# Chunk attention and token mixing: scores and mixing in quarters of the array, a permuted identity in E's transposes, steps and loads from a written table

## The chip, the core and the metric

The kernel runs on one core of a Trainium2 chip. The metric is the device time of one execution in microseconds (us); lower is better. A core has a matrix engine (TensorE, in the profile PE, its weight loads PEld), a vector engine (DVE), a scalar engine (ACT), GpSimd (POOL) and a queue engine (SP). Each runs its own instructions in order; semaphores order them among each other. PE writes only to PSUM, eight banks of 128 partitions by 512 words, from which DVE or ACT copy results to SBUF. Sixteen DMA engines carry data between the chip's memory and SBUF; here POOL issues the loads (they change float32 to float16 on the way), and SP issues the first two loads and all stores.

## What is computed

Per batch and head, attention inside chunks of 64 tokens, and then, per batch, a mixing of tokens whose weights come from the attention's output x (576 tokens, 512 columns):

```python
# q, k, v: (8 batches, 8 heads, 576 tokens, 64), chunks of 64 tokens
scores = scale * np.matmul(q_c, k_c.transpose(0, 1, 2, 4, 3))
scores = scores - np.max(scores, axis=-1, keepdims=True)
attn = np.exp(scores)
attn = attn / (np.sum(attn, axis=-1, keepdims=True) + 1e-09)
out = np.matmul(attn, v_c)
...
wq = x @ w_q
wk = x @ w_k
W_tok = scale * np.einsum('bsd,btd->bst', wq, wk)
mixed = np.einsum('bst,btd->bsd', W_tok, x)
return (np.maximum(mixed, 0.0) @ w_out).astype(np.float32)
```

The kernel never forms W_tok: with G = wk^T x (64 by 512 per batch), mixed is wq G.

## The kernel before

**Units.** A batch has 576 tokens: two *whole* units of 256 tokens (four chunks) and 64 tokens left over. The left-over chunks of two neighbouring batches, b and b + 1, form one *rest* unit. So there are 16 whole units and 4 rests, 20 in all, numbered in the order of `pairs`. Unit 0 is batch 0's first.

**Steps.** Each unit passes through the same steps; in brackets the line of the PE work, and the name that the table of the change gives it here.

- *Loads* (L263, L275, for rests L260, L271): q, k and v. A whole unit's q or k is one DMA of 256 KB (128 partitions, each with 8 heads and two neighbouring tokens); its v two of 128 KB. A rest has six DMAs of 64 KB.
- *Transposes of q and k* (tq, L402; rests L387): 16 per whole unit and tensor, 128 by 64 each, two column halves of the array side by side. They leave dims on partitions, two heads one above the other.
- *Copies*: k goes to `kt` in one copy. q goes to `qbd` in two copies of 64 partitions each, to the two diagonal blocks of a 128 by 128 tile whose other blocks were filled with zeros at the start. All simple copies carry line L318.
- *Scores* (S, L420): for each pair of heads and each chunk one matmul with the block-diagonal q as 128 by 128 weights and 64 columns of k; 16 per whole unit, 8 per rest.
- *Softmax*: maximum (mx, L433, DVE), subtraction (L444 or L440, DVE), exponent (L454, ACT). Two neighbouring tokens sit in one partition row after the load, so the keys come permuted; the subtraction's access pattern puts them back.
- *E* (L466): transposes of the exponents against an identity, then a copy `et`.
- *V* (L496): products with v, matmuls of 64 rows by 64 columns in quarters of the array, 65 columns of v with a column of ones that gives the sum. A whole unit has 32 in two groups that use four quarters; a rest has 16, each with its row half equal to its column half. Then DVE adds 1e-9, takes the reciprocal and multiplies (L508, L512, L522).
- *Projection*: transposes of x (xT, L538), product with w_q and w_k together (pj, L548), a transpose of wk (wkT, L565), each with a copy.
- *G* (L604), once per batch: ten matmuls over the batch's tokens, 128 by 64. Two copies put its halves side by side in rows 0 to 63 of `g16`, whose rows 64 to 127 are zero.
- *mix* (L645): four matmuls per whole unit with 128 by 128 weights out of `g16` and 256 columns (the lower half of the weights is the zeros). Then the relu (rm, L665 on ACT or L663 on DVE), whose access pattern puts the queries back in order.
- *out* (L679): product with w_out, four matmuls of 512 columns for each 128 tokens, a copy to `osb`, and the store (L693 to L699).

**Forms.** PE works in one of three forms: the full array, *tall* (128 rows by 64 columns: L402 and L604) and *quart* (64 by 64: L496). A change of form costs time.

**Order.** `plan` (L49) walks over all steps with a cost for each, a priority (unit number plus a lag for each kind, L163) and an estimate of when each load arrives. It picks for each engine what starts soonest, and gives each copy to DVE or ACT. The result is a fixed order on each engine. Where PE would wait early on, it inserts filler matmuls (`idle`, L712) with no use for the result, which keep PE busy and its clock up. Loads go out on POOL in the order of the units, q, k and v of each in turn, w_q and w_k after unit 1, w_out after unit 3. The order of the work on PE is thus fixed when the kernel is built; at run time an engine waits for whatever stands first on it.

## Time and profile before

| | |
|---|---|
| device time, median of three runs | 146.04 us (145.41 to 146.17) |
| span of the profiled execution, first to last instruction | 143.8 us |
| PE matmul, DVE, ACT, POOL busy | 127.5, 112.6, 101.3, 73.7 us |
| q0, loads issued by POOL: packets, MB | 78736, 14.29 |
| q1, loads and stores issued by SP: packets, MB | 7584, 10.49 |
| memory read, written | 29.62 MB, 9.44 MB |

The profile gives the span of the profiled execution only; the median of the runs shown lies 2.2 us above it. Columns of a row by line: line, engine, operation, output <- input, shapes, count; behind the bar the busy time in us and the mean of one in ns; behind the second bar the engine's idle time just before, and what ended it. Busy times of one engine can overlap a little (a matmul's latency runs into the next), so the distance from one start to the next tells more about PE than the mean of one. A DMA share above 1 means that packets wait for each other inside the sixteen engines.

### The profile page before, as it was taken

The page shows a single profiled execution, that of the slowest core. Times are in us where ns is not written, and L with a number is a line of the kernel's source. Part 1 is how long each engine was busy: PE and PEld are TensorE (multiplying, and loading weights), DVE is VectorE, ACT ScalarE, POOL GpSimd, SP SyncE. Part 2 cuts the span into 40 slices and gives each one's busy share as a digit, 9 for nine tenths or more (in the row PEclk, how much of TensorE's full clock was granted, in tenths as well). Part 3 has the DMA queues.
Part 4 walks back from the last instruction along what each step waited for, and adds up shares of the span by engine and source line. Part 5 has one row for each costly group of instructions (what it writes and reads, how often), then busy time and mean ns, then how long its engine had stood idle before and what let it go on. Part 6 is the DMA issues. An engine that isn't in the chain of part 4 may idle for free.

```text
span 143.8 us, 5196 instructions
## 1 busy us (share of the span) xinstructions
PE 127.5 (89%) x2204; PEld 90.8 (63%) x2204; DVE 112.6 (78%) x220; ACT 101.3 (70%) x182; POOL 73.7 (51%) x95
## 2 busy tenths in 40 slices
PE   5699799979799899998998999997999999997750
PEld 5565486566586776676675756786768766754310
DVE  6748988658989899897987899997999999933300
ACT  3333677457797899597978997867968687784740
POOL 7987997676499724551899526515960000000000
PEclk9999999999999999999999999999999999999998
DMA  3999999999999999999999999999999905527184
GB/s 88 268 176 155 129 165 184 169 175 175 156 133 173 234 218 175 208 247 239 86 151 195 216 241 207 213 257 168 125 181 229 270 22 152 140 75 197 31 250 111
DMA packets 86343, 25.11 MB, mean 175 GB/s; under 512 B 79152, under 2 KB 81712, under 8 KB 86320
## 3 DMA queue, kind: packets, MB, share of 16 engines
q0 software_dynamic: 78736, 14.29, 123.0%
q1 hardware_dynamic: 7584, 10.49, 23.7%
q8 instruction: 17, 0.28, 0.7%
q14 instruction: 6, 0.05, 0.1%
HBM read 29.62 MB, written 9.44 MB: 272 GB/s over the span
## 4 chain that ended last, share of the span: by engine, by line
PE 50%; DVE 15%; ACT 14%; DMA 10%; issue 4%; POOL 3%; POOLq 1%; ACTq 0%; DVEq 0%
PE ps L679 14%; PE ps L402 8%; DMA v_all<-in_v_dram 7%; PE ps L712 5%; PE ps L420 5%; DVE sh L444 4%; PE ps L496 4%; PE ps L538 4%; PE ps L548 3%; DVE qbd L318 3%; ACT qbd L318 3%; DMA osb<-in_q_dram 3%; ACT es L454 3%; PE ps L466 3%; DVE mx L433 2%
## 5 line engine op out<-in xcount | busy, mean ns | idle before, releaser
L679 PE MATMUL ps<-wo,rm 128*128 128x512 f16 x144 | 35.6, 379 | 0.7 <-ACT rm L665 0.7
L275 POOL DMA_DIRECT2D v_all<-in_v_dram x32 | 28.7, 912 | 3.1 <-DMA v_all<-in_v_dram 1.4
L433 DVE TENSOR_REDUCE mx<-ps 128x16 f32<-128x1024 f32 (+1 forms) x20 | 22.2, 1112 | 5.3 <-PE ps L420 4.2
L522 DVE TENSOR_TENSOR xs<-ps,rec 128x512 f16<-128x512 f32 x36 | 23.4, 685 | 0.1
L402 PE MATMUL ps<-ident,qk 128*64 128x128 f16 x512 | 20.7, 227 | 2.0 <-DVE qk L318 1.1
L318 ACT COPY osb<-ps 128x512 f32<-128x512 f32 x28 | 16.3, 586 | 7.9 <-PE ps L679 7.0
L454 ACT ACTIVATE es<-sh 128x1024 f16<-128x1024 f32 (+1 forms) x20 | 19.4, 970 | 3.2 <-DVE sh L444 1.7
L402 PEld LDWEIGHTS <-qk 128*64 128x64 f16 x512 | 16.4, 113 | 6.6 <-issue 3.7
L679 PEld LDWEIGHTS <-rm 128*128 128x128 f16 x144 | 12.6, 98 | 11.6 <-ACT rm L665 0.8
L444 DVE TENSOR_TENSOR sh<-ps,mx 128x1024 f32<-128x1024 f32 x16 | 19.6, 1223 | 0.4
L318 ACT COPY qbd<-ps 64x512 f32<-64x512 f32 (+1 forms) x30 | 15.9, 530 | 5.0 <-PE ps L402 3.0
L665 ACT ACTIVATE rm<-ps 128x1024 f16<-128x1024 f32 (+1 forms) x14 | 15.9, 1160 | 2.3 <-PE ps L645 2.3
L263 POOL DMA_DIRECT2D qk<-in_q_dram x15 | 13.6, 905 | 6.1 <-DMA qk<-in_q_dram 3.0
L263 POOL DMA_DIRECT2D qk<-in_k_dram x15 | 13.6, 906 | 5.1 <-DMA qk<-in_k_dram 5.1
L712 PE MATMUL ps<-ones 128*128 128x128 f16 (+1 forms) x72 | 13.8, 349 | 1.5 <-DVE ones L223 1.5
L420 PEld LDWEIGHTS <-qbd 128*128 128x128 f16 x288 | 10.8, 98 | 4.0 <-issue 1.8
L466 PE MATMUL ps<-ident,es 128*128 128x128 f16 x144 | 11.3, 219 | 1.9 <-ACT es L454 1.9
L420 PE MATMUL ps<-kt,qbd 128*128 128x64 f16 x288 | 11.6, 193 | 1.2 <-ACT kt L318 0.6
L538 PE MATMUL ps<-ident,xs 128*128 128x128 f16 x144 | 11.5, 219 | 0.4 <-DVE xs L522 0.4
L645 PE MATMUL ps<-wt,g 128*128 128x256 f16 (+1 forms) x96 | 10.6, 246 | 1.5 <-ACT g L318 1.0
L548 PE MATMUL ps<-xt,wqk 128*128 128x256 f16 (+1 forms) x80 | 11.2, 262 | 0.5 <-ACT xt L318 0.2
L271 POOL DMA_DIRECT2D v_all<-in_v_dram x8 | 5.4, 677 | 11.1 <-DMA qk<-in_k_dram 5.8
(54 smaller groups left out, 188.2 us busy)
## 6 DMA issues: line engine op xcount, KB each, us to landing
out_dram<-osb SPq DMA_DIRECT2D x40, 128.0 KB, 5.8
v_all<-in_v_dram POOLq DMA_DIRECT2D x32, 128.0 KB, 9.4
out_dram<-osb SPq DMA_DIRECT2D x16, 256.0 KB, 5.7
qk<-in_q_dram POOLq DMA_DIRECT2D x15, 256.0 KB, 8.5
qk<-in_k_dram POOLq DMA_DIRECT2D x15, 256.0 KB, 9.1
osb<-in_q_dram SPq DMA_DIRECT2D x1, 512.0 KB, 4.3
osb<-in_k_dram SPq DMA_DIRECT2D x1, 512.0 KB, 5.3
qk<-in_q_dram POOLq DMA_DIRECT2D x8, 64.0 KB, 8.9
```

The lines of the kernel that those rows point to most:

```text
L263: nc.gpsimd.dma_start(qk[u][:, t], rows)
L275: nc.gpsimd.dma_start(v_all[:, first[u] + i, :, 0:D], rows)
L318: (nc.vector.tensor_copy if eng == "DVE" else nc.scalar.copy)(to, of)
L402: nc.tensor.transpose(tp[half(o), j, :, r, :], of, ident[:])
L420: nc.tensor.matmul(sp[:, i, j, c, :], lhsT=st["qb", u][:, j, x].rearrange("p o s -> p (o s)"), rhs=st["kt", u][:, j, x * C : x * C + C], s ...
L433: nc.vector.tensor_reduce(mx[:], scores(), axis=AX.X, op=ALU.max)
L444: nc.vector.tensor_tensor(out=sh[:].rearrange("p x (g r) -> p x r g", r=R), in0=in_banks(bs, 512).rearrange("p i (x r g) -> p (i x) r g", ...
L454: nc.scalar.activation(es[:].rearrange("p x s -> p (x s)"), st["sh", u][:].rearrange("p x s -> p (x s)"), AF.Exp, scale=scale_attn,)
L522: nc.vector.tensor_tensor(out=to, in0=xp()[:, :, :, 0:D], in1=by, op=ALU.mult)
L538: nc.tensor.transpose(tx[:, f, i, :], xs[u][:, i, 2 * f : 2 * f + 2, :], ident[:])
L679: nc.tensor.matmul(op[c, :], lhsT=st["rm", u][:, f, i * P + c.start : i * P + c.stop], rhs=wo[:, f, :], start=(f == 0), stop=(f == NF - 1),)
L712: nc.tensor.matmul(ps[:, i, 0:cols], lhsT=ones[:, 0:P], rhs=ones[:, 0:cols], start=True, stop=True)
```

## The change

It touches almost every step. `plan`, its costs and its priorities are gone. In their place stand two texts. `ORDER` lists all 607 steps and the fillers, each with its engine (P for PE, V for DVE, S for ACT) and, for PE, the PSUM bank; `LOADS` lists POOL's loads. `w7` is a filler of 512 columns into bank 7, `n7` one of 128. Steps are numbered as they are added, unit by unit.

Ahead of unit 0's first transposes (7P0) stand 16 fillers, behind them 28 of w or n, so 44 in all:

```diff
+ORDER = """
+4V 5V 0S 1S w7 w7 w7 w7 n7 n7 n7 n7 n7 n7 n7 n7 n7 n7 n7 n7 7P0 2V 3S 8S w7 n7 n7 n7 n7 n7 n7 n7 n7
+9P1 10S 33P0 11P2 34V 12V 31P0 32S 13V w7 w7 n7 n7 n7 n7 n7 n7 n7 n7 55P0 35P4 56V 14S 36V 57P0 91P2
+15P3 92S 37V 89P6 16S 90S 58V 38S w2 n2 n2 n2 n2 n2 93P6 59V 113P4 94V 60S 39P5 61P0 21P2 95V 62S
+40S 17P0 114S 18V 22V 96S 45P4 23V 19V 41P6 24V 20V 97P2 42V 115P3 46V 43V 47V 48V 25P0 116S 44V n1
+n1 n1 63P4 26V 49P3 6S 64V 27P0 65V 50S 66V 98S 51P3 28S 67P1 103P4 68S 99P6 52S 104V 69P2 100V 105V
...
+456S 489P4 569V 462S 459P0 490V 463P1 570S 553P2 460S 549P6 571P4 554V 402S 550V 551V 457P0 555V
+552V 464S 572S 556V 491P1 458S 577P4 492V 573P2 467P6 578V 515P0 579V 574V 468S 575V 580V 557P1 516S
+493P6 469P7 576V 494S 558S 581P0 470V 517P1 559P2 518S 582V 519P1 560S 561P0 583P2 520S 465P3 521S
+584V 522V 585P2 562V 535P4 586S 529P6 466S 523P0 536V 587P2 524S 530V 537P3 588S 590V 525P0 538V
+589S 591P4 597P2 603P6 592V 527P1 604S 598S 605P6 528V 526V 533P2 606S 531P0 534S 595P1 532V 601P2
+596V 599P0 602V 593P1 600V 594S
+"""
+LOADS = """
+k1 q1 rq0b rq0a rk0b rk0a k3 q3 q4 v0b v0a v1b v1a k4 v3b rv0b rv0a wq wk v3a k5 v4b q5 wo rk1a v4a
+rq1b rk1b rq1a k6 v5a q6 v5b q8 rv1a rv1b k8 v6a v6b q9 k9 k11 q11 v8b v8a q12 v9a v9b k12 k14 v11b
+v11a q14 q15 v12b v12a k15 q18 v14b k16 q16 k17 v14a q17 k18 v15b v15a v17b v16b q19 v17a k19 v16a
+v18a v19a v19b v18b
+"""
```

Some numbers: 11, 35, 57 and 93 are the scores of units 0, 1, 2 and 3; 15 and 39 are E of units 0 and 1; 91 and 89 are unit 3's transposes of k and q, 113 and 115 unit 4's of q and k; 21 and 17 are V of unit 0; 553 and 549 are V of unit 18, 577 and 573 of unit 19. 587 is G of batch 7, the last; 537 and 525 are out steps, 591 and 597 the mixing of batch 7's units, 527 another out step.

`rests` are made of other batches now: (0, 1), (2, 5), (3, 6) and (4, 7), so that they come earlier in the order of units. The rests of the last three are loaded together, `rq1a` being the upper half of three rests' q in one DMA of 192 KB: twelve DMAs in place of 24. Unit 0's q and k come by SP in four halves in place of two.

```diff
+    both = [(0, 1)] + [(b, b + 3) for b in (2, 3, 4)]
...
+    order = const.tile([P, P], F16, name="order")
...
+    nc.gpsimd.tensor_copy(
+        order[:].rearrange("p (o g r) -> p o g r", o=2, r=R), ident[:].rearrange("p (o r g) -> p o g r", o=2, r=R)
+    )
```

q is copied once, as k is; nothing is filled with zeros for it:

```diff
-            def ev_q(eng, o):
-                to = qb[half(o), :, 0:nx, o, :].bitcast(F32)
-                copy(eng, to, of()[half(o)].rearrange("p j (x s) -> p j x s", x=nx))
...
+            def ev(eng, t=t, bk=bk):
+                tt = ring([P, HP, 4 * C], F16, "qk"[t] + "t4")
+                copy(eng, tt[:].rearrange("p j s -> p (j s)").bitcast(F32), in_banks(bk, 512)[:, 0])
+                st["qk"[t], u] = tt[:]
```

A rest's q and k are copied together (`qk2`). Scores become matmuls of 64 by 64 weights and 64 columns, head o of a pair in rows half o and output half o, 32 per whole unit and 16 per rest; the two banks of the result are taken in turn:

```diff
+    QUARTERS = ((0, 0), (1, 1), (1, 0), (0, 1))
...
-            for i in range(ni):
-                for j in range(HP):
-                    for c in range(2):
-                        x = 2 * i + c
+            for jj in range(ng // 4):
+                for c in range(2):
+                    for o, i in QUARTERS:
+                        j = jj if m is not None else 2 * i + jj
+                        s = slice((2 * i + c) * C, (2 * i + c) * C + C) if m is not None else half(c)
                         nc.tensor.matmul(
-                            sp[:, i, j, c, :],
-                            lhsT=st["qb", u][:, j, x].rearrange("p o s -> p (o s)"),
-                            rhs=st["kt", u][:, j, x * C : x * C + C],
+                            sp[half(o), i, jj, c, :],
+                            lhsT=st["q", u][half(o), j, s],
+                            rhs=st["k", u][half(o), j, s],
```

E's transposes multiply by `order`, the identity with its columns permuted, for whole units, so that queries come out in their order there and the relu reads and writes in order. V keeps its matmuls; their sequence over the quarters changes to that of `QUARTERS`.

The projection is split by halves of the tokens, with the weights in the order q, k for the first half and k, q for the second (`wqk` has a third block, a copy of the first, made by the step `again`): 8 matmuls of 128 columns for 4 of 256. So wq of the first half stands in rows 0 to 63 and wq of the second in rows 64 to 127. G is kept in both halves of the partitions, which takes three copies, one of 128 and two of 64 partitions, for two. Mixing then uses all four quarters, 16 matmuls of 128 columns (rests: 64 columns):

```diff
-            for o in range(2):
-                for f in range(2):
-                    for i, bb in enumerate(batches):
-                        s = slice(i * wide, i * wide + wide)
-                        c0 = (2 * o + f) * P
+            for f in range(NF):
+                for i, c in QUARTERS:
+                    g = st["g", batches[i % len(batches)]]
                     nc.tensor.matmul(
-                            ma[:, o, f, s],
-                            lhsT=st["g", bb][:, c0 : c0 + P],
-                            rhs=st["wt", u][:, s],
+                        ma[half(c), i, f, :],
+                        lhsT=g[half(i), f // 2 ^ i, f % 2 * P + c * C : f % 2 * P + c * C + C],
+                        rhs=st["wt", u][half(i), i * wide : i * wide + wide],
```

The number of buffers of most tiles changes by one or two (`xt` from 3 to 2, `osb` from 4 of 1024 words to 10 of 512).

More of the change, by code (lines that the diff above doesn't have):

```diff
@@ L317, in copy @@
+    QUART, TALL, FULL = "quart", "tall", "full"
+    PE, ACT, DVE, EITHER = "P", "S", "V", "SV"
     def copy(eng, to, of):
-        (nc.vector.tensor_copy if eng == "DVE" else nc.scalar.copy)(to, of)
+        (nc.vector.tensor_copy if eng == DVE else nc.scalar.copy)(to, of)
     st, xs = {}, {}
@@ L328, in ev @@
                 nc.vector.memset(part, value)
-        ready[key] = add("clr", CLEAR, {"DVE": sum(c for c in [0.3 * len(parts)])}, ev, [])
+        ready[key] = add("clr", len(parts), DVE, ev, [])
     for t in range(2):
@@ L336, in ev, with ev_again @@
                 to = qk[0][:, t, 4 * i : 4 * i + 4, :]
-                copy(eng, to.rearrange("p h e -> p (h e)"), wide_in[t][:, i, :])
-            cost = {"ACT": act(512, True), "DVE": 0.26}
-            ready.setdefault(("cast", t), []).append(add("cast", -9.0, cost, ev, [landed(("f32", t))]))
-    for n, t in enumerate(qbd[2:]):
-        clear(("qb", n + 2), [(t[:, j], 0.0) for j in range(HP)])
-    clear("ones", [(v_all[:, :, :, D : D + 1], 1.0)])
+                copy(eng, to.rearrange("p h e -> p (h e)"), wide[t, i][:])
+            key = ("ring", "osb", ("f", t, i))
+            s = add("cast", 0, EITHER, ev, [], makes=[key], uses=[key, ("load", f"f{t}{i}")])
+            ready.setdefault(("cast", t), []).append(s)
+    clear("ones", [(v_all[:, :, :, D : D + 1], 1.0), (v_rest[:, :, :, D : D + 1], 1.0)])
     clear("wkr", [(t[:], 0.0) for t in wkr])
-    for n, t in enumerate(g16):
-        clear(("g", n), [(t[half(1), :], 0.0)])
+    def ev_again(eng):
+        copy(eng, wqk[:, :, 2, :], wqk[:, :, 0, :])
+    ready["w"] = add("again", 0, EITHER, ev_again, [], uses=[("load", "wq")])
     def cleared(*keys):
```

662 lines of the change are left out of this document (286 added, 376 removed).

## The prediction

> **What bounds the kernel now.** I read the page first, its span and its busy shares.
>
> ```profile
> span 143.8 us, 5196 instructions
> ...
> PE 127.5 (89%) x2204; PEld 90.8 (63%) x2204; DVE 112.6 (78%) x220; ACT 101.3 (70%) x182; POOL 73.7 (51%) x95
> ```
>
> TensorE leads, but 89% is a mean over stages. So the busy time by stretch comes next (columns: stretch, its length, then busy time and instructions of PE, PEld, DVE, ACT, POOL; granted clock; DMA share; GB/s).
>
> ```profile
> 7.00:26.00 19.00, 17.95 (x312) 11.90 (x307) 15.18 (x27) 10.62 (x20) 16.37 (x21) 1.00 1.88 163
> 26.00:60.00 34.00, 31.63 (x586) 22.82 (x585) 28.38 (x54) 26.19 (x49) 22.59 (x28) 1.00 1.89 181
> 60.00:112.00 52.00, 49.12 (x946) 36.23 (x945) 47.23 (x95) 42.77 (x78) 28.48 (x35) 1.00 1.70 198
> 112.00:130.00 18.00, 17.50 (x277) 12.22 (x275) 15.16 (x32) 13.73 (x25) 0.00 (x0) 1.00 0.53 125
> ```
>
> From 26 to 130 PE is idle 2.4 + 2.9 + 0.5 = 5.8 us: it is the bound. The DMA share stays at 1.7 to 1.9 until 112 and then falls to 0.53: the loads run nearly full beside PE, so they are the next bound. Whether the first stretch is work, the order of PE's instructions tells (start, duration, engine, line, operation, count), with the row of the filler matmuls from the view by line:
>
> ```profile
> 1.46 3.70 PE L712 MATMUL ps<-ones 128*128 128x128 f16 x33 [1.46 <-DVE ones L223]
> 6.26 1.06 PE L402 MATMUL ps<-ident,qk 128*64 128x128 f16 x16 [1.10 <-DVE qk L318]
> ...
> 27.88 0.64 PE L402 MATMUL ps<-ident,qk 128*64 128x128 f16 x16
> ```
> ```profile
> L712 PE MATMUL ps<-ones 128*128 128x128 f16 (+1 forms) x72 | 13.8, 349 | 1.5 <-DVE ones L223 1.5
> ```
>
> Of 72 fillers 33 lie before the first transposes; the other 39 take 13.8 - 3.7 = 10.1 us, of which I count 9 as time that useful work could have had (a group's busy time runs on into the next). So there are three parts: a start short of data, a middle bound by PE, and an end.
>
> **Start.** At 27.88 PE transposes unit 4, after its fillers. That unit's loads stand here in POOL's order:
>
> ```profile
> 18.02 0.93 POOL L263 DMA_DIRECT2D qk<-in_q_dram  x1
> 18.89 0.94 POOL L263 DMA_DIRECT2D qk<-in_k_dram  x1
> ```
>
> They are the 20th and 21st loads on that queue, unit 3's the 15th and 16th. In the new table k3 and q3 are the 7th and 8th, q4 the 9th and k4 the 14th; at 0.7 to 0.9 us an issue they go out near 7, 8 and 12, some 6 us earlier, and unit 3's transposes, with q of unit 4, stand ahead of every product with v. POOL's one more copy (the ordered identity), no row of its own, I take at 0.4 us before the first load. What pays is v of unit 0, now 10th and 11th: ahead of it and with it go five loads of 256 KB, four of 64 and two of 128, 1.8 MB, at the 163 GB/s of the first stretch 11 us. From about 5, when SP's first loads end, that is 16. V of unit 0 is at 16.64 now, so it is hardly later, and in the table the steps S0 to S3 and E0 to E2 are queued before it and cover it. If v came late, everything behind it on PE would wait. The gain lies between nothing and the 9 us; the new table itself still has 28 fillers behind the first transposes (4 of 512 columns, 24 of 128; 2 us at the later rate). I take **-6.5 us**.
>
> **PE's own work.** Start to start, rows from the steady part:
>
> ```profile
> 78.17 0.60 PE L645 MATMUL ps<-wt,g 128*128 128x256 f16 x4
> 78.61 0.61 PE L538 MATMUL ps<-ident,xs 128*128 128x128 f16 x8
> ...
> 79.59 1.08 PE L402 MATMUL ps<-ident,qk 128*64 128x128 f16 x32
> 80.61 0.61 PE L548 MATMUL ps<-xt,wqk 128*128 128x256 f16 x4
> ...
> 83.88 0.64 PE L402 MATMUL ps<-ident,qk 128*64 128x128 f16 x16
> 84.45 0.50 PE L496 MATMUL ps<-v_all,et 64*64 64x65 f16 x32
> 84.88 1.04 PE L679 MATMUL ps<-wo,rm 128*128 128x512 f16 x4
> 85.85 0.64 PE L402 MATMUL ps<-ident,qk 128*64 128x128 f16 x16
> 86.42 0.44 PE L496 MATMUL ps<-v_all,et 64*64 64x65 f16 x16
> 86.79 1.04 PE L679 MATMUL ps<-wo,rm 128*128 128x512 f16 x4
> 87.67 0.63 PE L420 MATMUL ps<-kt,qbd 128*128 128x64 f16 x16
> 88.13 0.61 PE L538 MATMUL ps<-ident,xs 128*128 128x128 f16 x8
> ```
>
> An out step takes 0.87 before a full-array step (86.79 to 87.67) and 0.97 before a tall one (84.88 to 85.85): a change of form costs 0.1. Sixteen transposes take 0.57 before V, and 32 of them 1.02, so 0.45 + 0.12: again 0.12. V of a whole unit, 32 matmuls over four quarters, takes 0.43, less 0.12 is 0.31, 10 ns each. V of a rest, 16 matmuls whose row half equals their column half, uses two quarters: 0.37, less 0.12 is 0.25, 16 ns each.
> Scores: now 0.46 (87.67 to 88.13). The new ones are 32 matmuls of 64 columns, and q's and k's rows of head o go to output half o: two quarters of four. That is V's rest case, 32 x 16 = 0.50; +0.04 x 16, and +0.02 x 4 for rests: **+0.7**. Bounds: 32 x 10 ns, -2.2 in all; and, since every second one follows a matmul in its own quarter, that many weight loads in the open (priced with the slower rival), +15.
> Mixing: now 0.44 (78.17 to 78.61). The new 16 matmuls of 128 columns use all four quarters; 10 ns for 65 columns make 20 for 128, 0.32 or, if 10 ns holds an issue part, 0.24. I take 0.25: -0.19 x 16, and -0.1 x 4 for rests: **-3.4** (bounds -1.9 to -4).
> Changes of form: 92 in the order of before, 117 in the new table, since scores and mixing leave the full form: 25 x 0.12 = **+3.0**. Projections are cut into halves with the same columns, and rests' transposes widen by 64 columns: +0.2. Together PE gains nothing: **+0.5**.
> Two groups of weight loads, from the view by line (busy us and mean ns behind the bar):
>
> ```profile
> L645 PEld LDWEIGHTS <-g 128*128 128x128 f16 x96 | 7.3, 97 | 2.8 <-issue 0.9 <-DVE g L318 0.9
> L496 PEld LDWEIGHTS <-et 64*64 64x64 f16 x576 | 7.3, 107 | 4.4 <-issue 1.5 <-ACT et L318 1.3 <-ACT kt L318 0.2
> ```
>
> The Trainium skill, "TensorEngine Tiling (Array Packing)", Tile-to-Partition Mapping, Restrictions, speaks against the change: tiling by columns switches fast weight load off. The rows agree in sign: a load of 64 columns takes 107 ns in quarters, one of 128 in the full array 97. By the rule 896 loads (576 of scores, 320 of mixing) would cost 10 ns more each, and if bare PE's part would come out 9 us longer; by V's rows above, whose loads are of that kind and still allow 10 ns a matmul, nothing is added.
>
> **Copies out of PSUM.**
>
> ```profile
> L454 ACT ACTIVATE es<-sh 128x1024 f16<-128x1024 f32 x16 | 16.9, 1057 | 3.1 <-DVE sh L444 1.7 <-DVE den L508 1.2
> L318 ACT COPY osb<-ps 128x512 f32<-128x512 f32 x28 | 16.3, 586 | 7.9 <-PE ps L679 7.0 <-ACT rm L665 0.7
> L665 ACT ACTIVATE rm<-ps 128x1024 f16<-128x1024 f32 x11 | 14.4, 1316 | 2.3 <-PE ps L645 2.3
> L318 ACT COPY qbd<-ps 64x512 f32<-64x512 f32 x23 | 13.3, 579 | 4.8 <-PE ps L402 3.0 <-DVE qbd L318 1.3 <-ACT wkr L318 0.2
> L318 ACT CAST g<-ps 64x256 f16<-64x256 f32 x8 | 2.9, 368 | 2.6 <-DVE g L318 1.3 <-PE ps L604 1.0
> ```
> The whole units' 32 half copies of q (23 on ACT, 9 on DVE) cost 18.5 at ACT's 0.579; sixteen whole ones at 0.586, 9.4, replace them: -9.1. The rests' smaller ones and the fills of qbd and g I put at -4. The relu (rm) reads in order now; ACT's other 1024-wide pass in order takes 1.06 against 1.32: 12 x -0.26, -3.1. G has three copies for two: 8 x 0.37 = +3.0. Net -13 us on two engines of 214 busy together (112.6 + 101.3). While PE sets the pace this buys only shorter waits of PE: of the 5.8 us idle I take **-1.5** (bounds 0 to -4).
>
> **End.** Where PE waits last, then the last load, from the chain:
>
> ```profile
> 130.46 0.60 PE L604 MATMUL ps<-xs,wk 128*64 128x256 f16 x8
> 132.05 1.27 PE L645 MATMUL ps<-wt,g 128*128 128x256 f16 x16 [0.98 <-ACT g L318]
> 134.04 4.50 PE L679 MATMUL ps<-wo,rm 128*128 128x512 f16 x20 [0.72 <-ACT rm L665]
> ```
> ```profile
> 104.70 10.26 DMA v_all<-in_v_dram
> ```
>
> The new table puts two out steps between the last G and its mixing, and one behind that: 0.98 + 0.72 = **-1.7**. The sum of PE's part: 143.8 - 6.5 + 0.5 - 1.5 - 1.7 = **134.6**.
> But the loads hold as much data as before. Their last one lands at 104.70 + 10.26 = 115.0. In the table V of unit 18 waits for v18b, the last load, and behind it PE still has 13 out (0.87), 4 projections and 3 transposes (0.45), 7 mixings (1.4 together), 2 G (0.6), 4 V, 4 small ones (0.7 together) and 10 changes: 11.3 + 3.2 + 1.4 + 1.2 + 0.7 + 1.2 = 19.0. The last out ends now at 134.04 + 4.50 = 138.5 and the span at 143.8, 5.3 later: 24.3 behind the last load. The landing I put at 112.0: twelve issues fewer on POOL, which was busy without a break in one stretch,
>
> ```profile
> 70.00:80.00 10.00, 9.39 (x152) 6.59 (x150) 8.45 (x16) 8.58 (x17) 10.00 (x12) 1.00 1.57 157
> ```
>
> where DMA fell to 1.57; and 20 output tiles instead of some 23 stored ahead of it. At 198 GB/s three tiles of 256 KB are 4 us at most; half of that and 1 us for POOL make the 3. Bounds: 115 without any of it, 108 if the loads ran at 1.89 throughout (60 to 112 holds 52 x 0.19 / 1.89 = 5 us of slack, with 2 of the stores). So the span ends at 112.0 + 24.3 = **136.3**, later than PE's 134.6; the loads set the end. The runs shown have their median 2.2 above this span (146.04 against 143.8), so 138.5.
>
> **Rivals.** (a) **Loads go faster**, landing near 108; then PE's sum sets the end, with the whole 4 us of waits off: 132.1 + 2.2 = 134.3. For it: the share of 1.70; against it: it was no higher with POOL waiting on DMA. (b) **Earlier compute only feeds the DMA**: earlier outputs go out ahead of loads and the landing moves to 117: 141.3 + 2.2 = 143.5. For it: 1.89 leaves no room in the first 60 us. (c) **Slower: the scores run bare.** Place: the second matmul of each pair in one quarter waits for its weights. Sixteen such per unit over two quarters are 8 x 0.107 = 0.86 us, x 16, and half for 4 rests: 15.5 us. PE's sum becomes 150.1, with 2.2 152.3. It decides from 0.5 us a unit, where PE's sum passes 143.8. For it: V's rest alternates its quarters, so no row shows the same quarter twice running. Against it: sixteen transposes over two column halves take 0.45, 28 ns each for 128 columns, with loads fully hidden. The Trainium skill's rule on fast weight load, above, would push the same way. (d) **It does nothing**: order and quarters cancel, 146.
>
> **Numbers.** Forecast 0.45, (a) 0.20, (b) 0.16, (c) 0.13, (d) 0.06. Half a per cent is what a measurement of this kernel tells from no change. Faster: 0.45 + 0.20 + 0.16 = 0.81; same 0.06; slower 0.13. The range runs from 133.5, just below (a), to 146.5, which takes in (b) and (d); outside lie (c) and the far end of (a). The forecast's own range is 136 to 141 (landing 110 to 114.5).
>
> **What would show it.** Right: V of unit 18 released by the last v load near 112 and PE dense for 19 us behind it; unit 4's transposes before 22; scores at 0.50 start to start and mixing at 0.25; ACT and DVE together near 201 busy. Wrong: scores near 1 us; PE idle in the middle over 6 us; the last landing far from 112, which moves the end by as much.

## The result and the profile after

The changed kernel takes **155.38 us** (median of four runs, 154.87 to 156.07); the kernel before took 146.07 in runs beside it. The ratio is 1.0642 (95% interval 1.0601 to 1.0683): slower by 6%, where the prediction said 138.5. Some executions fell into a slower state of the chip and took some per cent longer; ratios leave these out, so that a ratio can differ a little from the quotient of two medians. The page after:

```profile
span 153.1 us, 6268 instructions
...
PE 125.1 (82%) x2768; PEld 89.4 (58%) x2768; DVE 105.2 (69%) x206; ACT 94.2 (62%) x175; POOL 67.6 (44%) x84
```

All engines work less than before, PE too (125.1 against 127.5), and yet the span is 9.3 us longer: what grew is PE's idle time. The stretches show where, in the columns of the prediction:

```profile
7.00:26.00 19.00, 13.38 (x375) 10.85 (x370) 13.86 (x25) 9.78 (x16) 15.53 (x20) 1.00 2.09 169
26.00:60.00 34.00, 29.50 (x602) 19.85 (x600) 23.89 (x46) 20.16 (x39) 22.10 (x25) 0.90 1.97 186
60.00:103.00 43.00, 34.94 (x873) 27.25 (x871) 30.28 (x61) 29.75 (x58) 23.60 (x27) 0.96 1.90 192
103.00:128.00 25.00, 24.05 (x611) 17.74 (x611) 21.41 (x41) 21.51 (x40) 0.00 (x0) 1.00 0.27 79
128.00:148.00 20.00, 18.33 (x278) 10.62 (x275) 14.25 (x28) 10.44 (x22) 0.00 (x0) 1.00 0.61 165
```

Up to 103 us, where the loads end (DMA share 1.90, then 0.27), PE idles 5.6, 4.5 and 8.1 us; from 103 to 128 one microsecond. Matmuls are no rarer there than before: 873 in 43 us are 20.3 a microsecond, where 946 in 52 were 18.2. What PE waits for, in the view of waits (line, releaser, total, times, longest):

```profile
PE ps L349 <- issue: 4.4, 3, 1.9
PE ps L425 <- issue: 2.9, 2, 1.7
PE ps L586 <- issue: 2.8, 2, 1.9
PE ps L317 <- ACT qk L253: 1.9, 1, 1.9
PE ps L317 <- issue: 1.7, 2, 1.1
...
PE ps L395 <- issue: 0.7, 1, 0.7
```

"Issue" means that nothing the profile records released PE: no semaphore, no bank. These rows sum to 12.5 us. In the kernel before the same view has a single such row:

```profile
PE ps L496 <- issue: 0.4, 1, 0.4
```

The order of PE's work shows that they do not stand at the start of a step but inside one: the row of 71.42 is the last 28 of a step's 32 scores matmuls.

```profile
64.68 0.40 PE L349 MATMUL ps<-kt,qt 64*64 64x64 f16 x13 [0.96 <-issue]
...
71.42 0.63 PE L349 MATMUL ps<-kt,qt 64*64 64x64 f16 x28 [1.51 <-issue]
...
84.36 0.53 PE L349 MATMUL ps<-kt,qt 64*64 64x64 f16 x21 [1.94 <-issue]
...
90.93 0.26 PE L425 MATMUL ps<-v_all,et 64*64 64x65 f16 x8 [1.16 <-issue]
...
97.12 0.31 PE L586 MATMUL ps<-wt,g 64*64 64x128 f16 x8 [0.91 <-issue]
...
103.87 0.49 PE L317 MATMUL ps<-ident,qk 128*64 128x128 f16 x11 [1.12 <-issue]
```

They strike any line, and they come with a beat: 64.68 to 71.42 is 6.74; 71.42 to 84.36 twice 6.47; then 6.57, 6.19, 6.75. Counted in that order of work, the five stretches hold 128, 256, 127, 128 and 128 matmuls (a trace can lack a record). In the middle of the 256, behind exactly 128 and 6.47 us after 71.42, stands a wait of 1.00 at 77.89; the view puts it down to ACT's relu, but that was done at 77.25, so 0.6 us of it look like one more wait for a block. The row of 103.87 is the last; the loads end there. One queue of the page explains the beat, here before and then after:

```profile
q8 instruction: 17, 0.28, 0.7%
```
```profile
q8 instruction: 21, 0.34, 0.9%
```

PE's program itself comes by DMA, in packets of 16 KB (0.28 MB over 17). A matmul is two instructions, the weights and the product, and 2 x 2204 / 256 = 17.2, 2 x 2768 / 256 = 21.6: a packet, called a block here, holds 256 instructions, 128 matmuls. The row in the table of queues gives the blocks a share of 0.9%, so their bytes are not what costs. **Theory F**: a block has to wait among the loads, on the same sixteen engines; while loads run, it takes some 6.5 us; PE waits wherever it uses up 128 matmuls faster. Between 64.68 and 71.42 it had 6.74 - 1.51 = 5.2 us of work for a block, later 6.57 - 1.16 = 5.4 and 6.75 - 1.12 = 5.6. The kernel before had 34.00 / (586 / 128) = 7.4 us a block from 26 to 60 and 52.00 / (946 / 128) = 7.0 from 60 to 112: on average a little more than the 6.5.

### The profile page after: what moved, and what is told of

The parts are those of the page before. It is cut to its first block, busy times and chain, and to the rows that moved or that the text cites. A ratio compares the mean times of both kernels' runs of the same rounds, so it can differ in the third digit from the quotient of the medians.

```text
span 153.1 us, 6268 instructions
## 1 busy us (share of the span) xinstructions
PE 125.1 (82%) x2768; PEld 89.4 (58%) x2768; DVE 105.2 (69%) x206; ACT 94.2 (62%) x175; POOL 67.6 (44%) x84
## 4 chain that ended last, share of the span: by engine, by line
PE 56%; DVE 12%; issue 11%; ACT 9%; DMA 5%; SPq 3%; DVEq 0%; ACTq 0%
PE ps L617 16%; PE ps L317 8%; PE ps L349 7%; PE ps L395 5%; PE ps L484 5%; PE ps L471 4%; PE ps L425 4%; DMA osb<-in_k_dram 4%; DVE sh L373 4%; DVE mx L362 4%; PE ps L586 3%; ACT rm L605 2%; ACT qt L253 2%; DVE xs L452 2%; ACT es L383 2%
## 5 line engine op out<-in xcount | busy, mean ns | idle before, releaser
L204 POOL DMA_DIRECT2D v_all<-in_v_dram x32 | 28.2, 886 | 10.4 <-DMA qk<-in_q_dram 2.6
L317 PE MATMUL ps<-ident,qk 128*64 128x128 f16 x512 | 21.0, 224 | 4.5 <-ACT qk L253 1.9
L317 PEld LDWEIGHTS <-qk 128*64 128x64 f16 x512 | 16.3, 111 | 8.4 <-issue 3.8
L253 ACT COPY osb<-ps 128x512 f32<-128x512 f32 x24 | 13.8, 589 | 7.4 <-DMA out_dram<-osb 3.8
L349 PE MATMUL ps<-kt,qt 64*64 64x64 f16 x512 | 11.9, 197 | 4.5 <-issue 4.4
L349 PEld LDWEIGHTS <-qt 64*64 64x64 f16 x512 | 10.1, 112 | 7.3 <-issue 6.4
L253 ACT COPY xt<-ps 128x512 f32<-128x512 f32 (+1 forms) x16 | 8.7, 548 | 8.6 <-PE ps L471 8.3
L425 PEld LDWEIGHTS <-et 64*64 64x64 f16 x576 | 8.2, 110 | 7.4 <-issue 5.5
L425 PE MATMUL ps<-v_all,et 64*64 64x65 f16 x512 | 9.2, 198 | 3.9 <-issue 2.9
L484 PE MATMUL ps<-xt,wqk 128*128 128x128 f16 (+1 forms) x160 | 11.3, 214 | 0.6 <-ACT xt L253 0.5
L253 ACT COPY qt<-ps 128x512 f32<-128x512 f32 x16 | 9.4, 590 | 3.6 <-PE ps L317 3.4
L586 PE MATMUL ps<-wt,g 64*64 64x128 f16 (+1 forms) x320 | 8.4, 224 | 3.9 <-issue 2.8
L395 PE MATMUL ps<-order,es 128*128 128x128 f16 x128 | 10.0, 220 | 1.8 <-ACT rm L605 1.0
## 6 DMA issues: line engine op xcount, KB each, us to landing
qk<-in_k_dram POOLq DMA_DIRECT2D x15, 256.0 KB, 10.7
```

The lines of the kernel that those rows point to most:

```text
L204: nc.gpsimd.dma_start(v_all[:, 2 * whole.index(u) + i, :, 0:D], of)
L253: (nc.vector.tensor_copy if eng == DVE else nc.scalar.copy)(to, of)
L317: nc.tensor.transpose(tp[half(o), j, :, r, :], of, ident[:])
L349: nc.tensor.matmul(sp[half(o), i, jj, c, :], lhsT=st["q", u][half(o), j, s], rhs=st["k", u][half(o), j, s], start=True, stop=True,)
L425: nc.tensor.matmul(to[half(c ^ i), n, x, :], lhsT=et[half(c), i, h // 2, h % 2, :], rhs=vals[half(c), h, 0:W], start=True, stop=True,)
L484: nc.tensor.matmul(pj[:, i * wide : i * wide + wide], lhsT=wqk[:, f, i : i + 2].rearrange("p i j -> p (i j)"), rhs=st["xt", u][:, f, i * w ...
```

## The experiments

Where an expectation names a theory by a letter, F is the one above; Q puts the loss on the 64 by 64 form of the new matmuls, T on the new table and its order. "Issue" stands for the sum of PE's waits put down to issue. Ratios are to the kernel before, in runs beside each.

### The stream of independent matmuls, with the loads

Only the loads of q, k and v, and 3072 quarter matmuls on constant data that wait for nothing:

```diff
+    for n in range(MATMULS):
+        i, c = ((0, 0), (1, 1), (1, 0), (0, 1))[n % 4]
+        nc.tensor.matmul(
+            ps[half(c), 4 * (n // 512 % 2) + i, 64 * (n // 4 % 8) : 64 * (n // 4 % 8) + 64],
+            lhsT=w16[half(i), 0:64],
+            rhs=w16[half(i), 64:128],
+            start=True,
+            stop=True,
+        )
```

> Not the computation: 3072 quarter matmuls of 64 columns on PE that depend on nothing, beside loads of q, k and v of the whole units as in the kernel, and then stores of zeros; all else is left out. Theory F: while the loads run PE gets some 128 matmuls (256 instructions) per 6.5 us, in bursts of under 2 us with waits on issue between them; behind the last load a block comes every 3 to 4 us. Theory Q: quarter matmuls run at one pace throughout, loads or not.

138.09 us in one run, issue 74.0 in 23 waits. PE's order of work; the DMA share is 1.87 from 60 to 80 us and 0.02 from 80 to 100, so the loads end at 80:

```profile
59.17 1.92 PE L77 MATMUL ps<-w 64*64 64x64 f16 x128 [4.82 <-issue]
65.64 1.92 PE L77 MATMUL ps<-w 64*64 64x64 f16 x128 [4.55 <-issue]
72.11 1.92 PE L77 MATMUL ps<-w 64*64 64x64 f16 x128 [4.55 <-issue]
78.58 1.92 PE L77 MATMUL ps<-w 64*64 64x64 f16 x128 [4.55 <-issue]
82.31 1.92 PE L77 MATMUL ps<-w 64*64 64x64 f16 x128 [1.81 <-issue]
85.76 1.92 PE L77 MATMUL ps<-w 64*64 64x64 f16 x128 [1.53 <-issue]
89.49 1.92 PE L77 MATMUL ps<-w 64*64 64x64 f16 x128 [1.80 <-issue]
93.49 1.92 PE L77 MATMUL ps<-w 64*64 64x64 f16 x128 [2.08 <-issue]
```

Every group has exactly 128 matmuls; 6.47 us from start to start beside the loads, 3.45 to 4.00 without. This is F in its pure form, on a chain that has no data to wait for. Q, one pace throughout, falls.

### More matmuls in the kernel before

The product with w_out in 16 matmuls of 128 columns instead of 4 of 512, 432 matmuls more and the same columns:

```diff
-                for f in range(NF):
-                    for c in cols:
+                for w in range(0, DM, DM // 4):
+                    for f in range(NF):
...
-                            rhs=wo[:, f, :],
+                            rhs=wo[:, f, w : w + DM // 4],
```

> The kernel before, with each out step written as 16 matmuls of 128 columns in place of 4 of 512: the same columns, 432 matmuls more (2636 in place of 2204), nothing else changed. Theory F (instruction fetch: PE's program arrives in blocks of 16 KB through the DMA engines that carry the loads, and more matmuls use a block up before the next is there): waits put down to issue appear in the middle of PE's steps while the loads run, with 1 us or so each, 4 to 10 us in all, and the time rises to 150 to 156 us. Theory Q (it is the 64 by 64 form of scores and mixing) and theory T (it is the new order): neither is in this kernel, so the time stays within 1 us of 146.

150.98 us, ratio 1.0364 (1.029 to 1.0438). Issue went from 0.4 to 4.4 us; the two largest rows, with the split product (L679) ahead:

```profile
PE ps L679 <- issue: 2.3, 3, 1.3
PE ps L466 <- issue: 1.0, 1, 1.0
```

So the kernel before turns slower by the number of matmuls alone, 5 us for 432 more with the same columns, with no quarter added, and at a clock of 0.994. Q and T had both said within 1 us of 146. PE is busy 1.7 us longer (129.2); with 4.0 more of issue that is the span's 5.1 (148.9 against 143.8) and a little more.

### The same count, without quarters, in the new table

First the new table with no quarters in scores and mixing: 16 full matmuls of scores a unit, taken from the one copy of q (so no diagonal copies either), and the mixing and projection of before; 2176 matmuls. Each of these scores sums two heads and two chunks, so that the results are not the reference's; what is kept is the number of steps and copies. Then the same with the product of w_out split as above; 2608.

```diff
-                            sp[half(o), i, jj, c, :],
-                            lhsT=st["q", u][half(o), j, s],
-                            rhs=st["k", u][half(o), j, s],
+                            sp[:, i, jj, c, :],
+                            lhsT=st["q", u][:, j, w : w + P],
+                            rhs=st["k", u][:, j, x * C : x * C + C],
```

> The changed kernel with the same steps, copies, order and loads, but 16 full matmuls for 32 quarter ones in a unit's scores, with no block-diagonal copies: each sums the scores of two heads and two chunks, so scores are not the reference's. Projection, mixing and G's copies are those of before. 2176 matmuls, as in the run with two q copies, whose second copies on DVE made PE wait. Theory F: waits on issue under 1 us, no new waits on DVE, span 136 to 142 us against 153.1. Theory T (the order is bad by itself): 150 or more, with waits of PE on other engines in the place of those on issue.

> The new table and its loads with no quarter matmul at all: scores summed over heads and chunks in 16 full matmuls (not the reference's scores), the mixing of before, and the output product cut from 4 matmuls of 512 columns into 16 of 128, as in the run of before with more matmuls. The kernel without the cut has 2176 matmuls and took 144.86 us with 2.9 us of waits on issue; this one has 2608. Theory F: 149 to 153 us, 7 to 11 us of waits on issue, all of them before the last load has landed. Rival Q: the forms of the matmuls matter and not their number: 144.5 to 146.5 us, under 4 us of waits on issue.

The first: 144.86 us, ratio 0.9935 (0.9868 to 1.0001), issue 2.9. F had put its span at 136 to 142 us with under 1 us of issue, and it is 143.1. Against the change, issue falls by 9.6 us and the span by 10.0 (153.1 to 143.1). The second: 151.11 us, ratio 1.0344 (1.0303 to 1.0384), issue 7.9, most of it here:

```profile
80.00 0.45 PE L474 MATMUL ps<-ident,xs 128*128 128x128 f16 x5 [1.49 <-issue]
86.29 0.22 PE L352 MATMUL ps<-kt,qt 128*128 128x64 f16 x2 [1.08 <-issue]
93.03 1.00 PE L616 MATMUL ps<-wo,rm 128*128 128x128 f16 x15 [1.05 <-issue]
99.77 0.19 PE L506 MATMUL ps<-ident,wt 128*128 128x64 f16 x1 [1.01 <-issue]
105.97 0.29 PE L428 MATMUL ps<-v_all,et 64*64 64x65 f16 x11 [0.88 <-issue]
```

Again 6.2 to 6.7 us from one to the next, and none behind the last row. The number alone, with full forms only, puts the loss back: 6.2 us for 432 matmuls. The rival that forms matter and not numbers (144.5 to 146.5) falls.

### Mixing alone or scores alone back to full

Two kernels between: quarter scores with full mixing (2464 matmuls), and full scores as above, not the reference's, with quarter mixing (2480).

```diff
-                    nc.tensor.matmul(
-                        ma[half(c), i, f, :],
-                        lhsT=g[half(i), f // 2 ^ i, f % 2 * P + c * C : f % 2 * P + c * C + C],
-                        rhs=st["wt", u][half(i), i * wide : i * wide + wide],
+                        nc.tensor.matmul(
+                            ma[:, o, f, i * wide : i * wide + wide],
+                            lhsT=st["g", bb][:, o, f * P : f * P + P],
+                            rhs=st["wt", u][:, i * wide : i * wide + wide],
```

> The changed kernel with projection, G's copies and mixing of before (4 projections and 4 full mixings a unit, zeros in the lower half of G); scores stay in quarters. 2464 matmuls. PE's own work grows by some 3 us (mixing 0.44 for 0.25). Theory F: a block of 256 instructions lasts longer, waits on issue fall from 12.4 to 4 to 7 us, and the time comes to 147 to 152 us. Theory T: waits on issue or not, no gain, 155 to 159.

> The changed kernel with 16 full matmuls for 32 quarter ones in a unit's scores (each sums two heads and two chunks, so the scores are not the reference's); mixing and projection stay in quarters and halves. 2480 matmuls, nearly as many as with the mixing of before (2464, 149.8 us span, of which some 3 us are PE's longer mixing). Theory F, where only the count matters: waits on issue of 6 to 8 us as there (7.1), span 146 to 149. Theory Q, scores' quarters being the cause: waits of 3 us or less.

151.69 us (ratio 1.0406, 1.0359 to 1.0453, issue 7.1) and 148.11 us (1.0174, 1.0118 to 1.023, issue 8.7). With the runs above, all in the new table:

| kernel | matmuls | us | issue, us |
|---|---|---|---|
| full scores, full mixing | 2176 | 144.86 | 2.9 |
| quarter scores, full mixing | 2464 | 151.69 | 7.1 |
| full scores, quarter mixing | 2480 | 148.11 | 8.7 |
| full scores and mixing, product split | 2608 | 151.11 | 7.9 |
| the change | 2768 | 155.38 | 12.5 |

Time goes up with the number, but not by it alone: the two in the middle, alike in number, are 3.6 us apart, near the 3.4 that quarter mixing was forecast to save. The issue waits of the first of them do not make up its 6.8 us.

### Fewer loads beside it

V of four units only is loaded and used for all, 24 loads of 128 KB fewer; the steps stay.

```diff
-        nc.gpsimd.dma_start(v_all[:, 2 * whole.index(u) + i, :, 0:D], of)
+        if whole.index(u) < 4:
+            nc.gpsimd.dma_start(v_all[:, 2 * whole.index(u) + i, :, 0:D], of)
```

> The changed kernel with v loaded for the first four whole units only; the other twelve use those values again, so that part of the input is left out (24 of 32 v loads). All steps of PE stay. Theory F: the loads end some 20 us earlier, and behind their end no wait on issue is left; the sum of these waits falls from 12.4 us to 6 to 9 and the span from 153 to 140 to 148. Theory Q: PE runs the same instructions and the waits stay near 12 us. Theory T: the waits stay, the span falls only where v was late (by 1 or 2 us).

150.66 us in one run, issue 8.4. These waits are 4.1 us less than in the change and the span 4.2 less (148.9, just above the 148 of the expectation). The loads end near 80 now, and so do the waits; first PE's order, then the stretches:

```profile
58.75 0.31 PE L587 MATMUL ps<-wt,g 64*64 64x64 f16 x13 [0.50 <-issue]
65.22 0.40 PE L350 MATMUL ps<-kt,qt 64*64 64x64 f16 x13 [1.17 <-issue]
71.69 0.63 PE L350 MATMUL ps<-kt,qt 64*64 64x64 f16 x28 [1.24 <-issue]
78.16 1.03 PE L396 MATMUL ps<-order,es 128*128 128x128 f16 x8 [1.84 <-issue]
```
```profile
60.00:80.00 20.00, 15.39 (x408) 12.24 (x405) 13.17 (x28) 13.85 (x29) 4.39 (x5) 0.95 1.58 195
80.00:103.00 23.00, 22.73 (x594) 17.97 (x592) 19.34 (x37) 18.71 (x38) 0.00 (x0) 0.97 0.20 60
```

6.47 us apart to the hundredth, and none behind 78.16. From 80 to 103 PE works 22.73 of 23.00 us, where the changed kernel stalled four times between 84 and 104. It is the loads beside it that make a block slow.

### Full scores with their diagonal copies, in the new table

As many matmuls as 2176, but with the block-diagonal q of before, its two copies on DVE and ACT, and then both on the engine that the table names for the one:

```diff
+                    for o in range(2):
+                        other = ACT if eng == DVE else DVE
+                        copy(eng if o == 0 else other, qb[half(o), :, :, o, :].bitcast(F32), of[half(o)])
```

> The changed kernel with its order, loads and permuted identity, but scores, projection and mixing in the forms of before (block-diagonal q in two copies, four full matmuls a mixing): 2176 matmuls in place of 2768. Theory F: the waits put down to issue shrink to under 2 us, the clock is back near 1.0, and the time falls to 136 to 143 us, below the kernel before. Theory Q: the same fall. Theory T: it stays at 150 us or more.

> As the run of the new table with the forms of before, but both half copies of q on ACT, one behind the other, so that no copy stands at the end of DVE's queue. 2176 matmuls. Theory F: no waits on issue; each q arrives 0.6 us later than in the changed kernel, hidden in part: 140 to 147 us. Theory T: 152 or more, as with the copies on DVE (157).

157.26 us (ratio 1.0769, 1.0678 to 1.086) with no issue wait at all, and 150.15 (1.0279, 1.0219 to 1.0339) with 0.4 us. F's times (136 to 143, and 140 to 147) were both missed, and the first lies where T had it, at 150 or more. In the first, DVE is busy 122.0 us and the granted clock is 0.948, where F had put it near 1.0; PE's waits went to the copies of q. Few instructions are thus no cure in a table that has no room for the second copy: with the same 2176 matmuls and one copy it was 144.86, 5.3 us less than the better of the two. As a test of F these two runs say one thing only: without the added instructions the issue waits are gone. How much of the time is the table's own they leave open.

### Other ways to fewer blocks, or to faster ones

Five q and k buffers instead of 11, to space the loads out:

```diff
-    NQK = 11
+    NQK = 5
```

> The changed kernel with 5 buffers for q and k in place of 11: the loads are held back by PE's transposes and spread over more of the run; nothing else changes, 2768 matmuls. Theory F: in the pauses of the loads a block comes in 3.5 to 5 us, waits on issue fall to 6 to 10 us, 149 to 155 us, unless data come late. If fetching is as slow beside fewer loads: no fall of these waits, 155 or more. Theory T: 155 or more, waits unchanged.

157.56 us (153.11 to 160.06). The issue of 14.6 us is that of the profiled execution, which was the longest of the four; of the shortest, which lies inside F's range, there is no profile. The spread is too wide for a verdict either way.

Then 8 full transposes instead of 16 tall ones for each of q and k, from loads that put the even and the odd tokens apart, in pieces of 256 bytes; 2512 matmuls, and 2208 with full mixing:

```diff
-                        for o in range(2):
-                            of = qk[u][:, t, 2 * j + o, r * D : r * D + D]
-                            nc.tensor.transpose(tp[half(o), j, :, r, :], of, ident[:])
+                        nc.tensor.transpose(tp[:, j, :, r, :], qk[u][:, t, r, 2 * j : 2 * j + 2, :], ident[:])
```

> The changed kernel with q and k of a whole unit loaded so that two heads of one token lie side by side (two DMAs of 128 KB in 256-byte pieces for one of 256 KB in 512-byte pieces), and 8 full transposes of 128 columns for 16 tall ones: 2512 matmuls, the same columns in the same time, all else kept. Theory F: waits on issue fall from 12.5 to 6 to 9 us; the loads take some 10 us more and end near 115, still ahead of their use: 147 to 151 us. If loads become the bound: 153 or more.

> The same with projection and mixing of before: 2208 matmuls, as many as the kernel before (2204), with the new table. Theory F: waits on issue of 1 to 4 us, 142 to 147 us, that is about the kernel before or below it. Theory T: 150 or more.

148.88 us (1.0234, 1.018 to 1.0288) and 149.96 (1.0267, 1.0214 to 1.0321). The issue waits fell further than F said, to 1.1 and 0 us for 6 to 9 and 1 to 4. The first time lies inside its range, the second 3 us above. In their place PE waits for the loads, here in the first run:

```profile
PE ps L318 <- DMA qk<-in_k_dram: 4.5, 6, 1.1
PE ps L426 <- DMA v_all<-in_v_dram: 3.8, 4, 2.2
```

Half the piece of memory at a time makes the loads themselves late; what the blocks gave was paid there. While PE waits for data the blocks have time to come, so these runs do not show what the number of matmuls alone does.

### The change under the planner of before

Is the table at fault? The planner of before charges each 256 instructions with a block of 6.4 us up to 100 us and 3.7 behind it (its constant `FETCH`). Three parts of the change were put into that kernel, each with the order that its planner makes: the permuted identity alone; all quarters with the one copy of q (2786 matmuls); and mixing in 8 matmuls of 64 rows by 128 columns, scores as before (2348).

```diff
-                nc.tensor.transpose(ep[:, x, :], es[:, x, :], ident[:])
+                nc.tensor.transpose(ep[:, x, :], es[:, x, :], (ident if m is None else order)[:])
...
-        n = add("S", u + LAG["S"], {"PE": 8 * ni * 0.0292}, pe_s, made, forms=FULL, takes=[bs], size=8 * ni)
+        n = add("S", u + LAG["S"], {"PE": 0.25 * ni}, pe_s, made, forms=QUART, takes=[bs], size=16 * ni)
...
-        n = add("mix", pri, {"PE": 4 * toks / 2350}, pe, [n for bb in batches for n in st["g_n", bb]], forms=FULL, takes=[bm], size=4 * len(batches))
+        n = add("mix", pri, {"PE": 0.11 * ni}, pe, [n for bb in batches for n in st["g_n", bb]], forms=ROWS, takes=[bm], size=8)
```

> The kernel before with one part of the change alone: E's transposes against the permuted identity, and the relu reading and writing in order (its cost in the planner lowered to match). The count of matmuls stays. All theories: the relu of a whole unit falls from 1.32 to 1.06 us on ACT; it is seldom what PE waits for, so 144.5 to 146.5 us; the planner may order differently by it.

> Before's planner, its loads and its order of steps, with the quarter matmuls: scores of 64x64 from one copy of the transposed queries, mixing in quarters, the permuted identity. Its planner charges each 256 instructions of the matmul engine with a block of 6.4 us while loads run, and places its steps by that. Theory F (the program's blocks come more slowly than the quarters use them up): the number of matmuls is about that of the changed kernel, so the planner's order can shift the waits but not remove the blocks: some 145 to 152 us, waits of PE put down to its own issue between 3 and 10 us. Rival T (the new table with its order is at fault, not the number of matmuls): the forecast's time of 137 to 142 us. Rival Q (quarter matmuls are dear by themselves, by their bare weight loads): above 152 us, with few waits put down to issue and the time of the scores steps above 1 us.

> Before's planner, loads, and block-diagonal scores; only the mixing is changed, to 8 matmuls of 64 rows by 128 columns a unit (as many steps, 4 matmuls more than before's 4 for a unit of one sequence and as many as before for a unit of two), the projection in two halves, the permuted identity, no clearing of the second half of the weighted values. Theory F: few instructions are added, so waits on issue stay under 2 us, and what the mixing saves (0.1 us or less a unit) shows: 143 to 146.5 us. Rival T (before's order is tuned to its own steps, and any other cost of a step upsets it): 147 to 150 us.

The identity: 146.03 us, ratio 1.0023 (0.9996 to 1.005), the same. The quarters: 163.07 us, 1.1071 (1.0996 to 1.1146). The rows: 148.62 us, 1.0164 (1.0127 to 1.0201). The page of the quarters:

```profile
span 160.7 us, 6322 instructions
...
PE 130.1 (81%) x2786; PEld 93.3 (58%) x2786; DVE 101.1 (63%) x201; ACT 97.1 (60%) x181; POOL 74.2 (46%) x96
```

Issue is 7.5 us there, inside F's 3 to 10 and less than the 12.5 of the new table, but PE idles 30.6 us in all, much of the rest in waits for other engines. That the order brings these by spreading the quarters to spare the blocks is likely, not shown. Theory T of that expectation, that the table loses and not the quarters (137 to 142 us), falls; so does F's figure of 145 to 152. Q has the time right, above 152, but it asked for few issue waits and for scores steps above 1 us; here a unit's scores take 0.50 from start to start between two mixings (68.60 to 69.10) and 0.62 with a change of form (86.75 to 87.37). The third lies in T's 147 to 150 us and not in F's 143 to 146.5: its issue waits were 3.0 us, above the 2 expected, for 144 matmuls more (in a profiled execution of 154.16 us, where the other three took 148.12 to 148.69, so the figure is loose). Whether those matmuls or the upset order made it slower is open. No version run here is faster than the kernel before by more than the measurement tells.

## Why the prediction was wrong

The step that failed is **"the sum of PE's part"**, 134.6: it counted time in the array, forms, fillers and waits for other engines, and had no term for the supply of instructions. Of the 5.8 us that PE idled it took 1.5 off; in fact issue waits of 12.5 us came on top. Its own sign of being wrong, "PE idle in the middle over 6 us", came: from 26 to 103 us PE idles 4.5 + 8.1 = 12.6 us. The change adds 564 matmuls, and the prediction took them as free beyond their 10 to 20 ns. What it needed was in the rows it quoted: 586 matmuls in 34.00 us are 7.4 us for 128, and the planner's code charges 6.4 for 256 instructions. With the forecast's 134.6 us over 2768 matmuls, a block has on average 134.6 / 21.6 = 6.2 us of work, under that charge. None of the rivals held it; the slower one put its 15.5 us on bare weight loads, another mechanism.

Point by point, against PE's part (134.6) and the span (153.1), 18.5 us apart:

- *Issue*: 12.5 us not in the sum. **Shown**, by the 128 matmuls between the waits, the stream, the split products and the fewer loads.
- *Start*, forecast -6.5. Fillers fell as forecast, from 13.8 us to 6.1 (x44), and unit 4's first transposes come at 18.23, the second at 23.91 against "before 22". But by 26 us PE has done only 32 transposes of q and k and 8 of E more than the kernel before (128 and 28 against 96 and 20), and no projection for its 8 matmuls. By the forecast's 0.45 us a step that is two sets of transposes and one of E gained and two projections lost, some 0.4 us in all. Of the 6.1 missing, 0.55 + 1.70 are issue waits; another 1.9 is the row of L317 on ACT above: k's second half landed late, at 2.33 + 6.06 = 8.4 us,

```profile
2.33 6.06 DMA osb<-in_k_dram
16.05 0.55 issue
21.47 1.70 issue
```

 (the chain that ended last, after). Loads that are asked for earlier shared the engines with it; that they made it late is argued, not tried.
- *Scores* and *mixing*. Both sizes were right:

```profile
28.48 0.69 PE L349 MATMUL ps<-kt,qt 64*64 64x64 f16 x32
29.10 0.64 PE L317 MATMUL ps<-ident,qk 128*64 128x128 f16 x16
...
110.56 0.42 PE L586 MATMUL ps<-wt,g 64*64 64x128 f16 x16
110.91 0.62 PE L484 MATMUL ps<-xt,wqk 128*128 128x128 f16 x8
```

 Start to start 0.62 and 0.35, less the forecast's 0.12 for the change of form: 0.50 and 0.23, where 0.50 and 0.25 were put. The rule of the Trainium skill ("TensorEngine Tiling (Array Packing)", Tile-to-Partition Mapping, Restrictions) that column tiling switches fast weight load off added nothing that these rows show, as the prediction chose; the slower rival's "scores near 1 us" did not come.
- *Copies*: DVE and ACT together 105.2 + 94.2 = 199.4 us, forecast near 201. Right in size.
- *Loads*: the last landing was put at 112.0 and came at 103, below the bound of 108 (by then PE had run 60 matmuls of the product with w_out, in the kernel before 76, so fewer stores went ahead of it; argued, not tried). The step "the loads set the end" was wrong as well: V of unit 18 ran at 127.30, long after its load. The 19.0 us of work that the forecast counted behind it came out (127.30 to 146.3); what had been late was PE.
- *End*, forecast -1.7. The waits of 0.98 and 0.72 are gone, but from the last product on it is 139.24 + 7.09 = 146.3 to 153.1, 6.8 us, where 5.3 were carried over; ACT waited 3.8 us for a store to free a buffer of the output:

```profile
139.24 7.09 PE L617 MATMUL ps<-wo,rm 128*128 128x512 f16 x32
...
146.41 0.58 ACT L253 COPY osb<-ps 128x512 f32<-128x512 f32 x1 [3.78 <-DMA out_dram<-osb]
```

- *Clock*. The mean granted clock fell from 0.996 to 0.961, with 0.83 in three stretches of 10 us (30 to 40, 50 to 60, 70 to 80); by stretches of 1 us it is 0.50 from 36 to 38, 53 to 55 and 73 to 76. At 8.52, 8.81 and 7.58 us of busy PE, 17% less clock is some 4.2 us. Each of the three begins within 1.5 us of the end of an issue wait (34.91, 51.19, 71.42), but behind the longest, which ends at 84.36, there is none. That the issue waits bring the clock down is **not shown**: the split product in the kernel before had 4.4 us of them at 0.994, the new table with both copies of q had none at 0.948, and with full scores from one copy the clock was 0.50 from 10 to 16 us, where PE's waits were for the first q and k. What in the new table costs the clock stays open.

Issue 12.5, the rest of the start 6.1 - 2.25 = 3.9, the end 1.5 and the clock 4.2 make 22.1, 3.6 more than the 18.5 to be explained: an estimate, in which clock and start are the loosest shares and may overlap. What is shown is the first and largest term. By itself the new table was worth little as well: without its quarters, and with issue down to 2.9 us, it ran at 0.9935 of the time before, not at the 0.95 of the forecast. So some 6 us of the miss (144.86 against 138.5) would be left without the added matmuls.

## What to carry to other kernels

Count instructions as well as time: for each stretch in which loads keep the DMA engines full, divide PE's time by its blocks of 128 matmuls, and compare with what a block takes there (here 6.5 us beside the loads, 3.5 to 4.0 without). Cutting full matmuls into quarters can save array time (here 0.44 to 0.23 us a mixing, nothing for the scores) and costs instructions; when the kernel stands at 7.0 us a block, the time saved comes back as waits. A wait put down to issue in the middle of a step, at a steady beat, is the sign to look for, and the queue of instruction packets shows its cause though its share is under 1%.

## What the runs showed of the hardware

- A block of 16 KB of instructions came every 6.2 to 6.75 us beside the loads (6.47 to 6.74 in the stream), where a load of q or k, sixteen times as large, took 9.5 and 10.7 us from issue to landing (medians of the changed kernel); with no loads every 3.45 to 4.00 us, still more than the 1.92 us in which PE runs the stream's 128 quarter matmuls. The Trainium skill, "Runtime: NRT & Kernel Launch", Instruction fetch mechanics, describes the blocks of 256 instructions as this trace shows them, and calls the cost of crossing one mostly hidden; here it is not, 12.5 us of 153.1 in the changed kernel and 74.0 of 135.7 in the stream.
- In the stream the first wait came behind 223 matmuls and ended at 6.59 us; every later one came behind 128, and the last group has 33 (223 + 22 x 128 + 33 = 3072). From this, as an estimate, about two blocks are there at the start.
- A granted clock of 1.000 in a profile can mean that no change of the clock is recorded. The view gives 1.000 for the whole stream, but its rows are those of a slow clock; first the stream, then the scores of the change:

```profile
L77 PE MATMUL ps<-w 64*64 64x64 f16 x3072 | 46.1, 238 | 75.2 <-issue 74.0
```
```profile
L349 PE MATMUL ps<-kt,qt 64*64 64x64 f16 x512 | 11.9, 197 | 4.5 <-issue 4.4
```

 The same form takes 194 ns in the change from 28 to 30 us, at 1.00, and 238 from 53.2 to 53.9, at 0.50; a weight load takes 109 and 153 there, in the stream 152. So the stream ran, by its durations, at half the clock from start to end, and says nothing on whether waits bring the clock down. The beat beside the loads is 6.5 us there as in the change, most of which runs at 1.00.
